# Sliding-window attention and a feed-forward layer on one core: batches 0 and 1 handled by token halves, with a new opening order

## The chip, the core and the metric

The kernel runs on one core of a Trainium2 chip. Its engines are TensorE (PE, with PEld for its weight loads), VectorE (DVE), ScalarE (ACT), GpSimd (POOL) and SyncE (SP, which only issues transfers). The metric is the device time of one execution in microseconds (us). Smaller is better.

## The reference

The input is `q`, `k` and `v` of 8 batches, 8 heads, 576 tokens and 64 numbers per head, all fp32. Each token sees the tokens at a distance of at most 32. The output is that of a feed-forward layer on 4608 tokens (512 to 2048 to 512).

```python
scores = scale * np.matmul(q, k.transpose(0, 1, 3, 2))
mask = np.abs(pos[:, None] - pos[None, :]) <= 32
scores = np.where(mask, scores, -1000000000.0)
attn = softmax(scores)                      # written out in the reference, with + 1e-09
x = np.matmul(attn, v)                      # heads joined: 4608 tokens x 512
h = x @ w_in
out = np.maximum(0.01 * h, h) @ w_out
```

## The kernel before

The whole program is written in the order in which each engine shall work; no scheduler moves anything. Each engine takes its instructions in that order, so a waiting instruction holds up all that stand behind it on its engine.

Heads are taken in 4 pairs (p = 0 to 3), so that a pair fills 128 partitions. Batches 0 and 1 are the "old" ones. Each is split into two halves of 288 tokens, and a step is one half of one pair: steps 0 to 3 are the first half of batch 0, 4 to 7 its second half, 8 to 15 batch 1. For a step, `score(i)` (10 small matmuls for batch 0 at L428, 5 for batch 1 at L435) writes a PSUM tile `ps`, ACT takes the exponential into `e` (L440), POOL multiplies it with a band mask into `prob` (L442), `sums(i)` (L466) adds up the rows on PE and DVE takes the reciprocal (L471, the longest DVE instruction), `product(i)` (L482) multiplies with `v`, and `scaled(i)` (L496, DVE) writes 288 columns of `xT`. There is one `ps`, so that the next score waits for the last exponential. `xT` is cut into 4 chunks of 128 rows, one for each pair. Batches 2 to 7 go another way (blocks of 64 tokens, transposes by DMA), from step 16 on (L380 to L411).

The feed-forward layer takes its tokens in groups. Groups 0 to 3 are the halves of batches 0 and 1 (288 tokens each). For each group there are 16 tiles `f`; a tile is 4 matmuls of 288 columns (`h_mms`, L520) and an ACT instruction (L531) into `gT`. The first 4 tiles of groups 0 and 1 are made chunk by chunk (`h_first`), so that they begin when pair 0 is there. 16 matmuls of 512 columns make one output tile of 128 tokens (`o_pair`, L609, for the first two, `o_tile`, L593, for the others). Between these, a plan with due times (`spend`) sets attention steps; its number `turn` counts the places between the matmuls from `o_pair` on.

In the opening, q and k of a pair come as a tile of 96 partitions with 6 tokens each (`load_qk`, L80, 288 KB per tile), v as two transfers of 144 KB per pair (L104), all issued by SP. They are cast to bf16 (`cast_qk`, L279 and L281), transposed on PE (6 transposes per tile, L327) and evicted by ACT (L335 for q, L341 for k). A first score thus needs both tiles of its pair whole. Queries stand with even and odd tokens apart. For batch 0 the keys are used from where ACT put them, for batch 1 DVE copies them into a block-diagonal tile `kbd` (L359). ACT or DVE cast v into a block-diagonal tile `vbd` (L287, L289). The weights come by 8 transfers that POOL issues: four quarters of w_in (4 tiles `f` each, L675) and four of w_out (L679), each 1 MB in memory, cast to bf16 on the way. `keep_busy` (L622) is matmuls whose result is not used.

`vf` and the tiles of `fload` have one buffer for each pair. Thus batch 1 is loaded when batch 0 has been cast; a POOL memset of one element (L76) holds its first load behind what POOL has done.

The opening's order around the first feed-forward matmuls reads (L744 ff.):

```python
    score(4)
    load_w_out(0)
    h0 = h_first(0)
    h = next(h0)
    keep_busy(h, HALF, 8)
    product(2)
```

Of the kernel before, what the change touches and what calls it, by code (L numbers as in the profile page):

```python
# [9 lines left out]
FP32 = mybir.dt.float32  # L10
# [6 lines left out]
def kernel(  # L17
# [14 lines left out]

    nc = tc.nc
# [12 lines left out]
    EVEN = HALF // 2  # L46
# [22 lines left out]
    def load_qk(b, p, behind=None):  # L69

        for into, src, name in ((qf, q, "qf"), (kf, k, "kf")):
            t = fload.tile([96, 2, RUN * D], FP32, name=f"{name}{p}")
            if behind is not None:
                behind.memset(t[0:1, 0, 0:1], 0.0)  # L76
                behind = None
            heads = src[b, 2 * p:2 * p + 2]
            if b < BY_DMA:
                nc.sync.dma_start(out=t, in_=heads.rearrange("a (p c) d -> p a (c d)", c=RUN))  # L80
            elif into is qf:
# [10 lines left out]

    vbuf = const.tile([128, NPAIR, 10 * D], FP32)
# [7 lines left out]
    def load_v(b, p):  # L101
        t = vf[b, p]
        for a in range(2):
            nc.sync.dma_start(  # L104
                out=t[64 * a:64 * a + 64],
                in_=v[b, 2 * p + a].rearrange("(c p) d -> p c d", p=64),
            )
# [17 lines left out]

    load_qk(0, 0)
    load_qk(0, 1)
    load_v(0, 0)
    load_qk(0, 2)
    load_qk(0, 3)  # L130
    for p in range(1, NPAIR):
        load_v(0, p)


    qb = const.tile([96, NPAIR, RUN, 2, D], BF16)
    kb = const.tile([96, NPAIR, RUN, 2, D], BF16)
# [5 lines left out]
    qT, kbd, vbd, qz, kz, vw, vw_two = [], [], [], [], [], [], []  # L142
    for t, at in zip(sets, (0, NPAIR * S)):
        qT.append(sets[0][:, at:at + NPAIR * S].rearrange("p (n s) -> p n s", n=NPAIR))
# [22 lines left out]
    def clear(t, p):  # L167
# [4 lines left out]

    mask = [const.tile([128, 2, 2, EVEN], BF16, name=f"mask{i}") for i in range(2)]
    nc.vector.memset(mask[0][:, 1, :, 0:16], 0.0)
    nc.vector.memset(mask[1][:, 1, :, 128:EVEN], 0.0)
# [7 lines left out]
        [((0, 0, 48), (2, 48, 64), (4, 112, 32)), ((1, 16, 64), (3, 80, 64))],  # L183
        [((4, 0, 32), (6, 32, 64), (8, 96, 48)), ((5, 0, 64), (7, 64, 64))],
    ]

    win = sets[1][:, N_SET - 384:].rearrange("p (c m i) -> p c m i", c=2, m=3)
    nc.gpsimd.memset(win, 1.0)
    for lo in (0, 64):
# [3 lines left out]
            base=0, channel_multiplier=-1, pattern=[[1, 2], [0, 3], [2, 64]],  # L193
# [3 lines left out]
            base=2 * W, channel_multiplier=1, pattern=[[-1, 2], [0, 3], [-2, 64]],  # L197
        )
    nc.gpsimd.memset(vbd[0][:, 3], 0.0)
    win_f = win.rearrange("p c m i -> p c (m i)")  # L200

    def make_mask(hf):
        lo = (16, 32)[hf]
        nc.gpsimd.tensor_copy(out=mask[hf][:, 0], in_=win_f[:, :, lo:lo + EVEN])
        lo = (16, 0)[hf]
        nc.gpsimd.tensor_copy(out=mask[hf][:, 1, :, lo:lo + 128], in_=win_f[:, :, 0:128])
# [49 lines left out]
    prob = const.tile([128, NPROB, 2, 2, EVEN], BF16)  # L256
# [3 lines left out]
    ps_v = ps[:, P0:P0 + 2 * HALF].rearrange("p (n c i) -> p n c i", n=2, c=2)  # L260
# [14 lines left out]
    def cast_qk(b, p, q_eng=None):  # L275
        for eng, src, dst in ((q_eng or nc.gpsimd, qf, qb), (nc.gpsimd, kf, kb)):
            to, tok = dst[:, p], src[b, p].rearrange("p a (c d) -> p c a d", d=D)
            if eng is nc.scalar:
                eng.activation(out=to, in_=tok, func=AF.Copy)  # L279
            else:  # L280
                eng.tensor_copy(out=to, in_=tok)  # L281

    def cast_v(b, p, on_act=False, heads=range(2), eng=nc.gpsimd):
        for a in heads:
            r = slice(64 * a, 64 * a + 64)
            if on_act:
# [31 lines left out]
    def transposes(b):  # L318

        for p in range(NPAIR):  # L320
            for which, src in (("q", qb), ("k", kb)):
# [17 lines left out]
                else:  # L339
# [5 lines left out]
                    if b == 0:  # L345
                        first_keys.append(kT)
                    else:
                        unplaced.append((b, p, kT))
# [555 lines left out]
```

## Time and profile before

| | |
|---|---|
| time, median of 3 runs (range) | 314.39 us (313.86 to 315.52) |
| time of the profiled execution | 314.13 us |
| span of its profile | 312.3 us |
| PE busy, share of the span | 298.2 us, 95% |
| DVE, ACT, POOL busy | 221.6, 212.6 and 199.1 us |
| PE busy in 0 to 10, 10 to 22, 22 to 40 us | 3.21, 10.03 and 17.64 us |
| first matmul of the feed-forward layer (L520) | 22.07 us |
| transfers of q0 (weights, by POOL) and of q1 (all else) | 4.19 and 44.84 MB written |

Times in a profile count from the start of the span; the time of the run is 1.8 us longer than the span. In the timeline a row is: start, length from the first instruction's start to the last one's end, engine, line, operation, tiles (written from read), shape, count, and in brackets the idle time before it with what ended that. The ends of matmuls are modelled. In the list of transfers the last number is the median time from issue to landing.

### The profile page before, as it was taken

The numbers are of one execution on the slowest core, as the hardware profiler recorded it, in microseconds if no ns is written. First come the engines' busy times: TensorE is split into PE (matmuls) and PEld (weight loads), VectorE is DVE, ScalarE is ACT, GpSimd is POOL, SyncE is SP. The second block draws the span as 40 slices with busy tenths as digits, with TensorE's granted clock in tenths as the row PEclk, the third lists the DMA queues.
The fourth block names the chain that finished last, engine by engine and source line by source line (L and its number), as shares of the span: only waits on it lengthen the run. The fifth ranks groups of instructions, "written<-read, shape, count | busy, mean of one in ns | idle before, by whom it ended". The sixth has DMA issues, their size and how long they took to land.

```text
span 312.3 us, 6748 instructions
## 1 busy us (share of the span) xinstructions
PE 298.2 (95%) x2516; PEld 194.8 (62%) x2545; DVE 221.6 (71%) x290; ACT 212.6 (68%) x434; POOL 199.1 (64%) x250
## 2 busy tenths in 40 slices
PE   1799999999999999999999999999999999999996
PEld 1577775585765858585959585858555555544643
DVE  3688959779768887898789767898679866743000
ACT  7687698583865858585949686858589548842731
POOL 7789936899799999488778357578947622110000
PEclk9999999999999999999999999999999999999999
DMA  8999999998999799989989995797950011001002
GB/s 181 224 217 227 268 249 198 204 216 143 211 216 216 145 266 174 206 174 251 198 145 186 257 230 101 163 209 144 206 129 0 33 67 41 0 36 68 34 28 75
DMA packets 122017, 49.47 MB, mean 158 GB/s; under 512 B 96256, under 2 KB 117504, under 8 KB 121984
## 3 DMA queue, kind: packets, MB, share of 16 engines
q1 hardware_dynamic: 117760, 44.84, 72.7%
q0 software_dynamic: 4224, 4.19, 8.0%
q8 instruction: 20, 0.33, 0.5%
q14 instruction: 13, 0.11, 0.1%
HBM read 36.70 MB, written 9.44 MB: 148 GB/s over the span
## 4 chain that ended last, share of the span: by engine, by line
PE 77%; POOL 10%; DMA 5%; ACT 3%; SPq 2%; issue 2%; DVE 1%; POOLq 0%; ACTq 0%; DVEq 0%
PE mm L520 34%; PE mm L593 31%; PE ps L380 3%; DMA kf<-in_k_dram 2%; PE mm L609 2%; POOL prob L387 2%; PE s L398 2%; POOL kb L281 2%; PE x L398 2%; POOL qb L281 2%; DMA set<-kb 1%; ACT set L287 1%; POOL prob L442 1%; DMA vbuf<-in_v_dram 1%; SPq L80 1%
## 5 line engine op out<-in xcount | busy, mean ns | idle before, releaser
L520 PE MATMUL mm<-xT,w_in_bf 128*128 128x256 bf16 (+3 forms) x956 | 133.2, 294 | 0.4
L593 PE MATMUL mm<-w_out_bf,gT 128*128 128x512 bf16 (+2 forms) x537 | 122.5, 373 | 1.3
L407 DVE RECIPROCAL r<-r 128x256 f32<-128x256 f32 (+1 forms) x56 | 94.9, 1696 | 37.3 <-ACT r L406 36.9
L520 PEld LDWEIGHTS <-w_in_bf 128*128 128x128 bf16 x960 | 91.4, 98 | 30.6 <-issue 0.6
L387 POOL TENSOR_TENSOR prob<-e,band 128x512 bf16<-128x512 bf16 (+1 forms) x56 | 62.6, 1117 | 56.0 <-ACT e L385 54.6
L593 PEld LDWEIGHTS <-gT 128*128 128x128 bf16 x560 | 52.0, 98 | 54.1
L531 ACT ACTIVATE gT<-mm 128x288 bf16<-128x288 f32 (+2 forms) x112 | 49.8, 479 | 12.3 <-PE mm L520 9.6
L385 ACT ACTIVATE e<-ps 128x512 bf16<-128x512 f32 (+1 forms) x56 | 32.4, 579 | 27.7 <-PE ps L380 27.0
L598 ACT ACTIVATE o_sb<-mm 128x512 f32<-128x512 f32 (+2 forms) x35 | 20.5, 585 | 38.5 <-PE mm L593 38.2
L554 ACT ACTIVATE gT<-mm 128x512 bf16<-128x512 f32 x64 | 35.7, 596 | 5.5 <-PE mm L520 4.2
L471 DVE RECIPROCAL r<-s 128x288 f32<-128x288 f32 x16 | 31.2, 1950 | 2.9 <-PE s L466 2.8
L281 POOL CAST kb<-kf 96x768 bf16<-96x768 f32 x32 | 27.2, 851 | 9.2 <-DMA kf<-in_k_dram 8.1
L411 DVE TENSOR_TENSOR xT<-x,r 64x256 bf16<-64x256 f32 (+1 forms) x56 | 24.3, 435 | 3.3
L411 DVE TENSOR_TENSOR xT<-s,r 64x256 bf16<-64x256 f32 (+1 forms) x56 | 24.3, 434 | 3.3
L442 POOL TENSOR_TENSOR prob<-e,mask 128x576 bf16<-128x576 bf16 x16 | 20.3, 1273 | 5.9 <-ACT e L440 4.9
L315 DVE COPY set<-kT 64x576 bf16<-64x576 bf16 x48 | 21.4, 446 | 2.1 <-DMA kT<-qb 1.2
L380 PEld LDWEIGHTS <-set 128*128 128x128 bf16 x216 | 16.7, 98 | 9.6 <-DMA set<-kb 0.4
L380 PE MATMUL ps<-set 128*128 128x128 bf16 x216 | 21.4, 219 | 0.2 <-DMA set<-kb 0.2
L281 POOL CAST qb<-qf 96x768 bf16<-96x768 f32 x24 | 19.6, 819 | 0.8 <-DMA qf<-in_q_dram 0.8
L294 POOL CAST set<-vbuf 128x640 bf16<-128x640 f32 x24 | 17.2, 716 | 3.1 <-DVE r L407 1.7
L398 PEld LDWEIGHTS <-set 128*128 128x128 bf16 x432 | 18.0, 98 | 0.5
L295 POOL CAST set<-vbuf 64x512 bf16<-64x512 f32 x24 | 14.8, 615 | 1.5
(84 smaller groups left out, 237.0 us busy)
## 6 DMA issues: line engine op xcount, KB each, us to landing
qf<-in_q_dram SPq DMA_DIRECT2D x32, 288.0 KB, 5.9
kf<-in_k_dram SPq DMA_DIRECT2D x32, 288.0 KB, 6.6
out_dram<-o_sb SPq DMA_DIRECT2D x35, 256.0 KB, 2.7
vbuf<-in_v_dram SPq DMA_DIRECT2D x15, 256.0 KB, 4.7
vbuf<-in_v_dram SPq DMA_DIRECT2D x16, 144.0 KB, 7.0
w_in_bf<-in_moe_w_in_dram POOLq DMA_DIRECT2D x4, 512.0 KB, 8.2
w_out_bf<-in_moe_w_out_dram POOLq DMA_DIRECT2D x4, 512.0 KB, 15.5
vbuf<-in_v_dram SPq DMA_DIRECT2D x10, 192.0 KB, 4.5
```

The costliest lines, as they stand in the source:

```text
L281: eng.tensor_copy(out=to, in_=tok)
L380: nc.tensor.matmul(sc[:, :, w], kz[b % 2][:, p, 64 * m:64 * m + 128], tok[:, :, :, at:at + 32], start=True, stop=True,)
L385: nc.scalar.activation(out=e[:, 0:n], in_=ps[:, lo:lo + n], func=AF.Exp, scale=scale)
L387: nc.gpsimd.tensor_mul(pr, e[:, 0:n], band.rearrange("p w c i -> p (w c i)")[:, 0:n])
L398: nc.tensor.matmul(x[:, a, w], vw[b % 2][:, p, m, a:a + 2].rearrange("p n d -> p (n d)"), pr[:, a, w], start=True, stop=True,)
L407: nc.vector.reciprocal(r[:, 0:n], r[:, 0:n])
L411: nc.vector.tensor_mul(xT[rows, p, t0:t0 + n].rearrange("p (w i c) -> p w c i", i=32, c=2), x[rows, a].rearrange("p (w c i) -> p w c i", c ...
L471: nc.vector.reciprocal(r, s)
L520: nc.tensor.matmul(h[:, 0:n], w_in_bf[:, c, ts(f, 128)], xT[:, c, t0:t0 + n], start=(c == 0), stop=(c == DMC - 1),)
L531: nc.scalar.activation(out=to, in_=h, func=AF.Prelu, alpha=0.01)
L554: nc.scalar.activation(out=gT[:, f - 1:f + 1, t0:t0 + 256], in_=hh.rearrange("p (f t) -> p f t", f=2), func=AF.Prelu, alpha=0.01,)
L593: nc.tensor.matmul(o[:, lo:hi], gT[:, f, t0:t0 + 128], w_out_bf[:, f, lo:hi], start=(f == 0), stop=(f == FFC - 1),)
```

## The change

For batches 0 and 1, a load is now one half of one pair: 48 rows of q and 64 (first half) or 32 (second half) rows of k in one tile of 112 or 80 partitions (`load_half`), by two transfers. v comes as 5 blocks of 64 tokens and later the other 4. All first halves of a batch are loaded ahead of its second halves. One cast, 6 transposes, one eviction and, for batch 1, two DVE copies serve a half tile. Tokens stand in natural order in `qk`, the masks, `prob` and `gT`. `score` leaves out the masking, which `mask_out` does where it is called, for step 0 on DVE. The opening is a new list: `warm_up` (37 matmuls of 128 columns) in place of `keep_busy`; both masks at the start; two clears (`clear_half(0, 0, .)`) on DVE at the start, which stood on ACT and POOL beside `o_pair`; two tiles (`h_first(0, 2)`) begun early in place of four; the four w_in transfers each behind one POOL masking or cast; the four w_out transfers and the loads of batch 1 among the second half's steps; POOL's making of `band`, two clears and DVE's `clear_half(1, .)` at other places. In batch 1, half tiles are transposed behind tiles 5, 8, 11 and 14 of group 1, and at turns 6, 8, 11 and 13 (before: pairs behind tiles 7 and 11 and at turns 1 and 5). In the last lines of the diff, `transpose_part` is the transposes of a half tile and its two copies into `kbd`, and `cast_part` is the cast of the half tile of pair 2, then 3, on DVE.

```diff
+    QROWS, KROWS = 48, (64, 32)
+    def load_half(b, p, hf, behind=None):
+        t = load_tile(p, ("qf", "kf")[hf])
+        if behind is not None:
+            behind.memset(t[0:1, 0, 0:1], 0.0)
+        k0, kn = 384 * hf, KROWS[hf]
+        for src, row, t0, n in ((q, 0, HALF * hf, QROWS), (k, QROWS, k0, kn)):
+            nc.sync.dma_start(
+                out=t[row:row + n],
+                in_=src[b, 2 * p:2 * p + 2, t0:t0 + RUN * n].rearrange(
+                    "a (p c) d -> p a (c d)", c=RUN),
+            )
+        halves[b, p, hf] = t[0:QROWS + kn]
...
-    load_qk(0, 0)
-    load_qk(0, 1)
-    load_v(0, 0)
-    load_qk(0, 2)
-    load_qk(0, 3)
+    load_half(0, 0, 0)
+    load_half(0, 1, 0)
+    load_v(0, 0, 0, 5)
+    load_half(0, 2, 0)
+    load_half(0, 3, 0)
     for p in range(1, NPAIR):
-        load_v(0, p)
+        load_v(0, p, 0, 5)
+    for p in range(NPAIR):
+        load_half(0, p, 1)
+        load_v(0, p, 5, NB)
...
+    def transposes(b, p, hf, tag="mm"):
+        n = QROWS + KROWS[hf]
+        pool = mmps if tag == "mm" else xps
+        tp = pool.tile([128, RUN, 112], BF16, name="tp", tag=tag)[:, :, 0:n]
+        for c in range(RUN):
+            nc.tensor.transpose(
+                tp[:, c], (qb, kb)[hf][0:n, p, c].rearrange("p a d -> p (a d)"), ident[0:n, 0:n],
+            )
+        at = halves_at(hf)
+        nc.scalar.activation(
+            out=qk[b][:, p, at:at + RUN * n].rearrange("p (i c) -> p i c", c=RUN),
+            in_=tp.rearrange("p c i -> p i c"), func=AF.Copy,
+        )
...
     def h_out(g, f, h):
         t0, n = GROUPS[g]
-        to, h = gT[:, f, t0:t0 + n], h[:, 0:n]
-        if g < 2 * BY_DMA:
-            to = to.rearrange("p (i c) -> p i c", c=2)
-            h = h.rearrange("p (c i) -> p i c", c=2)
-        nc.scalar.activation(out=to, in_=h, func=AF.Prelu, alpha=0.01)
+        nc.scalar.activation(out=gT[:, f, t0:t0 + n], in_=h[:, 0:n], func=AF.Prelu, alpha=0.01)
...
-        if i == OLD - 2:
-            for a in range(2):
-                clear_half(0, 2, a, nc.gpsimd)
+        if OLD <= i < OLD + NPAIR:
+            clear_half(1, (i - OLD) // 2 * 2, i % 2, nc.vector)
...
+    warm_up(24)
+    clear_half(0, 0, 0, nc.vector)
+    clear_half(0, 0, 1, nc.vector)
+    cast_half(0, 0, 0, nc.vector)
+    make_mask(0)
+    make_mask(1)
+    cast_half(0, 1, 0, nc.vector)
+    transposes(0, 0, 0)
+    warm_up(5)
+    score(0, nc.vector)
+    transposes(0, 1, 0)
+    warm_up(8)
+    cast_v(0, 0, nc.vector, hi=5)
+    cast_half(0, 2, 0, nc.gpsimd)
+    load_w_in(0, 512)
+    mask_out(0)
+    score(1)
+    sums(0)
+    transposes(0, 2, 0)
+    product(0)
+    scaled(0)
+    mask_out(1)
...
+    score(3)
+    h0 = h_first(0, 2)
+    h = next(h0)
+    sums(2)
+    transposes(0, 0, 1)
+    mask_out(3)
+    load_w_in(1024, 1536)
+    product(2)
+    scaled(2)
+    next(h0)
+    cast_v(0, 3, nc.scalar, nc.gpsimd, hi=5)
+    cast_half(0, 1, 1, nc.scalar)
+    score(4)
+    sums(3)
+    next(h0)
+    transposes(0, 1, 1)
+    mask_out(4)
+    load_w_in(1536, 2048)
+    cast_half(0, 2, 1, nc.scalar)
+    cast_half(0, 3, 1, nc.gpsimd)
+    product(3)
+    scaled(3)
+    next(h0)
+    score(5)
+    sums(4)
+    next(h0)
+    transposes(0, 2, 1)
+    cast_v(0, 0, nc.scalar, nc.gpsimd, lo=5)
+    mask_out(5)
...
+    f = 2
+    for i, n in zip(range(NPAIR, 2 * NPAIR), (2, 3, 4, 5)):
+        for f in range(f, f + n):
+            h_tile(0, f)
+        f += 1
+        if i < 6:
+            score(i + 2)
+        product(i)
+        scaled(i)
         if i < 7:
             sums(i + 1)
+        if i == 4:
+            transposes(0, 3, 1)
+        if i < 6:
+            mask_out(i + 2)
+        if i < 7:
+            cast_v(0, i - 3, nc.scalar, nc.gpsimd, lo=5)
+            load_w_out(i - 4)
+        if i == 4:
+            halves_of(1, 0, nc.gpsimd)
+    load_w_out(3)
+    for p in range(NPAIR):
+        load_v(1, p, 0, 5)
+    halves_of(1, 1)
+    for p in range(NPAIR):
+        load_v(1, p, 5, NB)
+    for p in range(NPAIR):
+        nc.gpsimd.memset(kbd[1][:, p], 0.0)
+    clear_half(0, 2, 0, nc.vector)
+    clear_half(0, 2, 1, nc.vector)
+    cast_half(1, 0, 0, nc.vector)
+    cast_half(1, 1, 0, nc.vector)
+    for p in (0, 1):
+        nc.gpsimd.memset(vbd[1][:, p], 0.0)
     for p in (2, 3):
         nc.vector.memset(vbd[1][:, p], 0.0)
     for _ in h_first(1):
         pass
+    for _ in band_parts:
+        pass
...
     for f in range(4, FFC):
         h_tile(1, f)
-        if f in (7, 11):
-            second_pair((f - 7) // 4)
+        if f in (5, 8, 11, 14):
+            transpose_part((f - 5) // 3)
+            if f < 11:
+                cast_part((f - 5) // 3 + 2)
         if f == 13:
             score(8)
+            mask_out(8)
```

310 lines of the change are left out of this document (117 added, 193 removed).

## The prediction

> **What bounds the kernel now.** I read the page's slices first, then its list of transfers, the stretches, the waits of PE, the timeline of the first 46 us, and the chain.
>
> ```profile
> PE   1799999999999999999999999999999999999996
> w_in_bf<-in_moe_w_in_dram POOLq DMA_DIRECT2D x4, 512.0 KB, 8.2
> w_out_bf<-in_moe_w_out_dram POOLq DMA_DIRECT2D x4, 512.0 KB, 15.5
> ```
>
> ```profile
> 22.00:62.00 40.00, 39.18 (x360) 26.40 (x362) 32.33 (x42) 30.43 (x63) 29.78 (x33) 1.00 1.18 231
> 62.00:104.50 42.50, 42.10 (x364) 28.89 (x367) 33.47 (x42) 28.52 (x67) 39.10 (x55) 1.00 1.08 194
> ```
>
> The fields are the stretch, its length, then busy time of PE, PEld, DVE, ACT and POOL, clock, DMA share and GB/s. From 22 us on PE is the bound: it stands only 0.82 of 40 us, then 0.4 of 42.5 (there POOL is busy 92%). So the change can gain only ahead of 22 us (PE busy 13.2 of 22), and can lose anywhere.
>
> ```profile
> 4.14 1.53 DVE L281 CAST qb<-qf 96x768 bf16<-96x768 f32 x1 [1.79 <-DMA qf<-in_q_dram]
> 8.30 0.66 PE L428 MATMUL ps<-set,kT 64*64 64x96 bf16 x10
> 9.87 1.27 POOL L442 TENSOR_TENSOR prob<-e,mask 128x576 bf16<-128x576 bf16 x1 [0.57 <-POOL kb L281]
> 11.09 0.93 POOL L675 DMA_DIRECT2D w_in_bf<-in_moe_w_in_dram  x1
> 18.83 0.43 PE L428 MATMUL ps<-set,kT 64*64 64x96 bf16 x10
> 22.07 1.14 PE L520 MATMUL mm<-xT,w_in_bf 128*128 128x288 bf16 x8
> 23.54 1.55 POOL L679 DMA_DIRECT2D w_out_bf<-in_moe_w_out_dram  x2
> 35.52 2.53 DVE L281 CAST qb<-qf 96x768 bf16<-96x768 f32 x2
> 38.11 1.15 DVE L788 MEMSET set<- 128x576 uint32 x2
> 41.12 0.56 DVE L281 CAST qb<-qf 96x768 bf16<-96x768 f32 x1
> 44.09 1.03 PE L609 MATMUL mm<-w_out_bf,gT 128*128 128x512 bf16 x3
> ```
>
> In these timeline rows the opening is a chain: cast, transposes, eviction, score, masking, sums, and each link waits for the one before. The same DVE cast takes 1.53 us beside a POOL memset and 0.56 us without one. Ten score matmuls take 0.66 us early, 0.43 at 18.83.
>
> ```profile
> PE tp L327 <- DVE qb L281: 6.4, 2, 5.7
> PE s L466 <- POOL prob L442: 1.4, 2, 1.2
> PE ps L380 <- DMA set<-kb: 0.2, 1, 0.2
> ```
>
> The waits of PE (sum, number, longest) say the same: 6.4 of its idle time is for the first casts. Places to gain are the opening's chain and, at most 0.6 us, the wait for a transposing DMA at 104.5.
>
> **A. The chain of batch 0's first half.** A half tile is 112 rows of 3 KB, 336 KB where a q tile had 288. Four tiles land between 4.14 and 8.48 (the DVE and POOL casts that wait for them), 1.45 us each, so the first casts can start at about 4.4 instead of 4.14. But POOL's memset L199 (4.21, 1.06) remains, and the cast should again end near 5.7: no gain. The two clears now on DVE (0.54 each at 7.83 and 8.53) fit into its 1.79 us of waiting. Then 6 transposes instead of 12 and one eviction (0.65 us for 576 columns, about 0.73 for 672): score(0) at 7.3 instead of 8.30. Its masking goes to DVE, for which there is no row: POOL needs 1.27; DVE's scaled copy of half as many columns 0.46; I take 0.7, nearer to DVE's row. sums(0) then stands at 9.6 (before 11.20). Two more rounds of exponential, masking and the PSUM tile `ps` at 2.4 to 2.5 us each (before 3.3 and 4.0, with two casts per pair between them) give sums(2) at 14.6 instead of 18.50, and product(2) at 15.8.
>
> **B. The first matmul of the layer.** It needs the first quarter of w_in. POOL issues that behind its cast of pair 2's half tile, which lands at about 8.5 (1.2 MB from the start, at the 0.2 MB per us of the tiles above), and casts for 0.82: issue 9.3 instead of 11.09. With the page's median of 8.2 us it lands at 17.5. The other end: landings of quarters three and four lie 2.5 us apart in the trace, so a quarter alone could be there at 13; and if loads crowd it, 19. So PE stands about 1.7 us, and the first matmul comes at 17.5 instead of 22.07: 4.5 us earlier.
>
> The Trainium skill ("DMA: Bandwidth & Descriptors", section "Queues, rings and completion order") says that each DMA engine goes round its queue rows packet by packet. By that rule POOL's quarter shares the engines with SP's loads as long as these last, as the 8.2 us show; the sum stays as it is, and without the rule it would be that of rival 2.
>
> **C. Group 0.** Those 4.5 us are not kept, because the second half's steps are now the chain. mask(4) runs on POOL from about 19.0 to 20.3; behind it stand on POOL the fourth w_in issue (0.8), a cast of a k tile (0.82) and half a v cast (0.4), then mask(5) (1.27): 23.7. sums(5) follows at 23.8. From there PE has work: 12 tiles of 4 matmuls at 0.49 (16 matmuls from 38.90 to 40.86), 0.24 for each of six sums and products, 0.33 for a score, 0.22 for transposes, 7.9 in all, and some 0.3 of waits: group 1's first matmul at 32.0, before 34.04. Gain 2.0.
>
> **D. Group 1 up to the output pair.** Before: 16 tiles 7.84, six tiles of transposes 1.56, a score 0.24, one wait for ACT 0.42, in all 10.06; the rows say 10.0 (34.09 to 44.09). Now: 7.84, four half tiles at 0.29 (0.26 for 96 rows), 0.24, 0.33: 9.6, so 41.6. But the transposes now come from tile 5 on, and their casts stand on DVE behind scaled(7) (to 33.5), the clears L254 that were on POOL (1.3 beside its memsets), two casts (2.53 at 35.52, beside POOL's memsets), two memsets (1.15), copies. The first half tile is cast at 36.1 and wanted at 35.3; the third at about 39.8 to 40.5, wanted at 39.5 after that wait. I take 1.0 of waiting (0.5 to 1.7): 42.6 instead of 44.09, gain 1.5. Four smaller half tiles (0.22 each) follow later where one pair (0.51) did: gain 1.1 carried on.
>
> **E. w_out.** The four issues stand on POOL behind mask(6), mask(7) and v casts: about 26, 28.8, 30 and 30.8, where they were 23.54, 24.34, 26.35 and 28.45. Before, a quarter was there 10.2 us after the first issue and the others 4.65 us apart (landings in the trace, 33.75 to 46.90). Now 34.5 to 36.2 for the first, so the third between 43.8 and 45.5; `o_pair` wants it at 44.6, the fourth at 49.7. Wait 0 to 1.6, I take 0.5.
>
> **F. The output tiles up to 62 us.** ACT gets 16 v casts of 0.4 instead of 8 of 0.69 and four more evictions of about 0.55, less a clear of 1.2: hidden, ACT is busy 30 of 40. DVE's key copies (384 columns, 0.33 each by 0.45 for 576) move to turns 6 to 13, between its reciprocals: 0.3 of waits, an estimate.
>
> **G. After 62 us.** POOL loses two clears (1.06 each) and three parts of `band` (about 2.0) there, where it runs at 92%: I give 0.3 of the 0.6 us at 104.5. DVE gets four clears, 2.8 us, over four steps at 79% busy: hidden; if not, up to 0.7.
>
> **The rest** costs nothing on the path: `warm_up`'s matmuls stand ahead of the first cast and in waits of A; natural order changes only how ACT and POOL walk their tiles, which the PE-bound stretches hide (L531 takes 0.48 us, a tile on PE 0.49; were it slower in the new order, ACT would set the pace, but the order gets plainer); the doubled number of SP's load issues has slots of 0.4 us free.
>
> **Sum.** -1.1 (A to D) +0.5 (E) +0.3 (F) -0.3 (G) = -0.6 on the profiled execution of 314.13: 313.5. The median of the runs is 0.26 above the profiled one: 313.8. A measurement of this kernel can tell about 0.5%, 1.57 us, from no change; so this is "the same" (312.8 to 316.0).
>
> **Rivals.** 1. *The late w_out becomes the wait (slower).* If batch 1's loads, issued at nearly the same moment, take more of the DMA than before (the first w_in quarter took 8.2 us under load against 2.5 apart when nothing else ran), the third quarter lands near 48 instead of 45, and `o_pair` stands 3.4 us instead of 0.5: 316.7. For it: DMA share 1.18 in 22 to 62. Against: both requests start later together. It decides from a landing of the third quarter at 47.3.
>
> 2. *The opening's gain is kept (faster).* If the first quarter comes by 15.8, as the 2.5 us apart would allow, PE does not stand; the POOL chain of C starts 1.2 us earlier, group 1 at 31.0; DVE's queue then waits 0.5 rather than 1.0, and w_out comes in time: 313.8 - 1.0 - 0.5 - 0.5 = 311.8. Against: while batch 0 is loaded the trace shows 8 us, not 2.5.
>
> 3. *A slow PE after the stand.* If PE stands longer than 1.7 us, what follows may go at the early price (0.66 for 0.43) for a few us; PE isn't alone the bound there, so about +0.7: 314.5. It would want first matmuls of the layer at twice 0.12 us each.
>
> The Trainium skill ("TensorE: Matmul & The Clock Gate", section "What's actually happening") has a clock at half rate until about 3.4 us of sustained work, and again after such an idle window. The rows 0.66 and 0.43 agree in kind; by it `warm_up` would make score(0) and score(1) some 0.2 us shorter each, and the sum 313.6 at best.
>
> 4. *No gain in the opening*: if the score of step 1 or 2 waits for ACT (two evictions, an exponential and casts in one queue), sums(2) is near 18 again and group 1 starts at 33.5: with D to G 315.3.
>
> **How the numbers follow.** Forecast 0.42, rival 1 0.18, rival 2 0.25, rival 3 0.06, rival 4 0.09. Around 313.8 the open costs (D 0.5 to 1.7, E 0 to 1.6, F and G some 0.7 either way) make about 1.3 each way, which is the likeliest case's own range, 312.5 to 315.1; 0.06 of its 0.42 fall below 312.8. Faster: 0.25 + 0.06 = 0.31. Slower: rival 1, half of rival 4 (its 315.3 with the same open costs) and 0.01 of rival 3: 0.24. Same: the rest, 0.45. The range reaches over rival 2 with 1.0 of the open costs below it, and over rival 1 with 0.5 above it: 310.8 to 317.2.
>
> **What would show it.** Right: first score near 7.3, sums(0) at 9.6, first layer matmul at 17 to 18.5 with a wait on w_in ahead of it, group 1's first matmul near 32.0, o_pair's near 42.6 with waits for DVE's casts before it, group 2's first within 1 us of before's 61.8. Wrong: a first layer matmul before 16.5 or after 20, a third w_out quarter after 47, a PE wait over 2 us anywhere between 22 and 62, or a PE wait after 62 that before does not have; and a reciprocal chain on DVE that sets the pace from 62 on, for which I put nothing.

## The result and the profile after

The changed kernel takes 325.96 us (median of 4 runs, 323.91 to 326.59), the kernel before 314.22 us (4 runs, 313.86 to 315.52): ratio 1.0355 [1.0298, 1.0411]. It is slower by 11.7 us where 313.8 us were forecast. The profiled execution took 325.49 us and has a span of 323.8 us (before: 314.13 and 312.3).

The page of after, its slices and its weight transfers:

```profile
PE   5659987997899999999999999999999999999996
PEclk9758999999999999999999999999999999999999
w_in_bf<-in_moe_w_in_dram POOLq DMA_DIRECT2D x4, 512.0 KB, 6.7
w_out_bf<-in_moe_w_out_dram POOLq DMA_DIRECT2D x4, 512.0 KB, 10.9
```

Before, the row of PE was full from the third slice (of 8.1 us) on; now it has holes up to the eleventh, and PE's clock is reduced in slices two to four. Both weight loads land faster than before (8.2 and 15.5 us then), so they are not what is missing. The stretches of after (length, busy PE, PEld, DVE, ACT, POOL, clock, DMA share, GB/s) give their size:

```profile
0.00:10.00 10.00, 5.54 (x71) 4.50 (x71) 5.06 (x16) 7.50 (x9) 6.96 (x17) 1.00 0.64 169
10.00:22.00 12.00, 6.12 (x69) 4.16 (x69) 6.89 (x6) 6.20 (x11) 6.55 (x9) 0.60 1.08 196
22.00:62.00 40.00, 35.52 (x328) 24.24 (x326) 29.96 (x43) 27.88 (x65) 29.07 (x35) 0.95 0.96 186
62.00:104.50 42.50, 39.04 (x333) 25.72 (x330) 31.25 (x41) 27.68 (x65) 30.67 (x39) 1.00 1.05 199
```

PE now stands 4.5 us of the 40 from 22 on (before 0.8), and 3.5 of the next 42.5 (before 0.4). From 22 us on no other engine is fuller than before, so none of them became the bound: they wait too. In the first 10 us the DMA engines are emptier than before, where this stretch reads

```profile
0.00:10.00 10.00, 3.21 (x34) 2.35 (x35) 4.76 (x14) 7.45 (x9) 6.96 (x17) 1.00 0.91 194
```

so there the loads are short of transfers given out, not of DMA engines (share 0.64 against 0.91). The waits of PE (sum, number, longest) say what it stood for:

```profile
PE tp L345 <- ACT kb L292: 4.3, 1, 4.3
PE tp L345 <- POOL kb L294: 2.0, 1, 2.0
PE tp L345 <- DVE qb L294: 1.9, 2, 1.2
```

Apart from the 2.2 us that PE waits ahead of its very first matmul, these are the longest of the opening and of batch 1, and all three are transposes (`tp`) that wait for the cast of a half tile: two of a second half (`kb`), one of batch 1's first half (`qb`). The timeline of after shows what those casts wait for themselves:

```profile
6.96 0.43 PE L434 MATMUL ps<-set 64*64 64x96 bf16 x10 [0.54 <-ACT set L349]
7.27 3.96 SPq L116 DMA_DIRECT2D vbuf<-in_v_dram  x6
11.92 0.64 SPq L98 DMA_DIRECT2D kf<-in_k_dram  x1
19.10 0.84 ACT L292 ACTIVATE kb<-kf 80x768 bf16<-80x768 f32 x1 [4.45 <-DMA kf<-in_k_dram]
19.99 0.58 PE L345 MATMUL tp<-ident,kb 80*128 80x80 bf16 x6 [4.31 <-ACT kb L292]
20.82 0.69 PE L530 MATMUL mm<-xT,w_in_bf 128*128 128x288 bf16 x2
37.12 9.95 SPq L116 DMA_DIRECT2D vbuf<-in_v_dram  x8
47.12 1.27 SPq L98 DMA_DIRECT2D kf<-in_q_dram  x1
54.28 0.82 POOL L294 CAST kb<-kf 80x768 bf16<-80x768 f32 x1 [2.77 <-DMA kf<-in_k_dram]
55.16 0.39 PE L345 MATMUL tp<-ident,kb 80*128 80x80 bf16 x6 [2.05 <-POOL kb L294]
59.94 0.54 SPq L77 DMA_DIRECT2D qf<-in_q_dram  x1
```

An SP row gives when transfers are given out, and the number in brackets how long an engine stood and for what. The second half of pair 0 is given out by SP at 11.27 (q) and 11.92 (k) as transfers 17 and 18, lands at 17.13 and 19.01, is cast by ACT at 19.10 and transposed at 19.99, and only then can the first matmul of the layer follow at 20.82, although its quarter of w_in (issued at 10.04) had landed at 16.16. In batch 1 the same happens behind eight v transfers: SP gives out the first second half at 47.12. And the loads of batch 2, which stand behind all of this in SP's queue, begin at 59.94; in the trace of before they begin here:

```profile
49.10 0.58 SPq L82 DMA_DIRECT2D qf<-in_q_dram  x1
```

So batch 2's loads start 10.84 us later. More than half of this arises ahead of batch 1, whose first load is given out at 25.19 before and at 31.64 after:

```profile
25.19 0.32 SPq L80 DMA_DIRECT2D qf<-in_q_dram  x1
31.64 0.32 SPq L98 DMA_DIRECT2D qf<-in_q_dram  x1
```

SP has nothing to give out from 24.49 to 31.64, because the POOL memset that releases batch 1 comes at 31.53 (before: 25.07). So 6.45 us are the later release, and 4.39 are the giving out of batch 1, which takes 28.30 us for 32 transfers where it took 23.91 for 16.

How far after lags behind before at fixed points of the program, from the two timelines:

| point | before, us | after, us | lag | forecast |
|---|---|---|---|---|
| first layer matmul | 22.07 | 20.82 | -1.2 | -4.5 |
| group 1's first | 34.1 | 37.2 | +3.1 | -2.0 |
| first of `o_pair` | 44.1 | 48.1 | +4.0 | -1.5 |
| group 2's first | 62.1 | 68.7 | +6.6 | -0.3 |
| an output tile at the end of the stretch from 62 us | 100.6 | 111.7 | +11.1 | |
| end of the span | 312.3 | 323.8 | +11.5 | -0.6 |

From 112 us on the lag hardly changes: nearly all of the loss lies in the opening and its echo.

### The profile page after: what moved, and what is told of

It is laid out like the page before. It is cut to its first block, busy times and chain, and to the rows that moved or that the text cites. A ratio compares the mean times of both kernels' runs of the same rounds, so it can differ in the third digit from the quotient of the medians.

```text
span 323.8 us, 6901 instructions
## 1 busy us (share of the span) xinstructions
PE 301.9 (93%) x2561; PEld 195.6 (60%) x2561; DVE 225.7 (70%) x303; ACT 213.1 (66%) x444; POOL 197.3 (61%) x251
## 4 chain that ended last, share of the span: by engine, by line
PE 67%; DMA 13%; POOL 8%; SPq 5%; ACT 3%; issue 2%; DVE 1%; POOLq 0%; ACTq 0%; DVEq 0%
PE mm L601 30%; PE mm L530 29%; DMA vbuf<-in_v_dram 6%; DMA kf<-in_k_dram 6%; PE ps L386 3%; POOL prob L393 2%; PE s L404 2%; SPq L128 2%; PE x L404 2%; DMA kT<-qb 2%; SPq L98 2%; SPq L116 2%; POOL prob L452 1%; POOL kb L294 1%; POOL qb L294 1%
## 5 line engine op out<-in xcount | busy, mean ns | idle before, releaser
L530 PE MATMUL mm<-xT,w_in_bf 128*128 128x256 bf16 (+3 forms) x960 | 135.3, 295 | 0.1
L601 PE MATMUL mm<-w_out_bf,gT 128*128 128x512 bf16 (+2 forms) x560 | 124.6, 373 | 0.0
L606 ACT ACTIVATE o_sb<-mm 128x512 f32<-128x512 f32 (+2 forms) x35 | 20.5, 585 | 36.2 <-PE mm L601 35.9
L294 POOL CAST kb<-kf 96x768 bf16<-96x768 f32 (+1 forms) x29 | 24.0, 830 | 6.5 <-DMA kf<-in_k_dram 5.3
L452 POOL TENSOR_TENSOR prob<-e,mask 128x576 bf16<-128x576 bf16 x15 | 19.2, 1277 | 12.1 <-ACT e L446 11.7
L294 POOL CAST qb<-qf 96x768 bf16<-96x768 f32 (+1 forms) x25 | 20.6, 822 | 4.2 <-DMA qf<-in_k_dram 2.0
L349 ACT ACTIVATE set<-tp 128x672 bf16<-128x672 bf16 (+1 forms) x16 | 10.4, 650 | 9.4 <-PE tp L345 9.2
## 6 DMA issues: line engine op xcount, KB each, us to landing
w_out_bf<-in_moe_w_out_dram POOLq DMA_DIRECT2D x4, 512.0 KB, 10.9
```

Of the source, the lines that this page charges most:

```text
L294: eng.tensor_copy(out=to, in_=src)
L530: nc.tensor.matmul(h[:, 0:n], w_in_bf[:, c, ts(f, 128)], xT[:, c, t0:t0 + n], start=(c == 0), stop=(c == DMC - 1),)
L601: nc.tensor.matmul(o[:, lo:hi], gT[:, f, t0:t0 + 128], w_out_bf[:, f, lo:hi], start=(f == 0), stop=(f == FFC - 1),)
```

## The experiments

Theory 1: the doubled number of SP's transfers is the cost; SP gives them out one after another, so that everything behind them in the queue is late. Theory 2: their order is the cost (second halves behind v, batch 2 behind both). Theory 3: the casts that ACT now does in order hold up its exponentials. Lags are those of the table, against the kernel before.

**split_before**: the kernel before, with every load of batches 0 and 1 in two pieces.

```diff
-                nc.sync.dma_start(out=t, in_=heads...)
+                for lo in (0, 48):
+                    nc.sync.dma_start(out=t[lo:lo + 48], in_=rows[lo:lo + 48])
...
+            for lo, hi in ((0, 5), (5, NB)):
+                nc.sync.dma_start(out=t[64 * a:64 * a + 64, lo:hi], in_=rows[:, lo:hi])
```

> The kernel before, with every load of batches 0 and 1 cut into two transfers (q and k tiles into two times 48 rows, v into 5 and 4 blocks), nothing else moved. Theory 1 (count: SP gives out transfers one after the other, 0.45 to 0.6 us each, and the ninth waits until the first has landed, so half-sized transfers keep fewer bytes under way): batch 0 lands some 3 us or more later, batch 1 and so batch 2 too, 317 to 322 us. Theory 2 (place: the second halves stand behind v and behind a POOL memset at 31.5) and theory 3 (ACT stands on a cast) have no part in this kernel: 313.5 to 315.5 us.

Measured: 324.24 us (324.07 to 324.36), ratio 1.0329 [1.0304, 1.0354]. Same bytes, same order, same compute, and 10 us are lost. SP is done with batch 0 at 20.98 instead of 15.34 and begins batch 1 at 28.68 instead of 25.19. The first layer matmul lags by 3.9, group 1 by 10.8, and that stays. In its waits of PE:

```profile
PE x L483 <- ACT set L288: 7.4, 3, 3.6
```

That is `product` waiting for the casts of v, which are the last of batch 0's loads. PE's mean clock is 0.72 from 22 to 40 us, so a slower PE may be part of the 10 us; that was not separated. For the kernel before theory 1 holds, more strongly than expected.

**whole_v**: after, with v loaded whole (24 transfers per batch instead of 32).

```diff
-    load_v(0, 0, 0, 5)
+    load_v(0, 0)
...
-        load_v(0, p, 5, NB)
```

> The kernel after, with v of batches 0 and 1 loaded whole again (8 transfers per batch in place of 16), at the place of the first parts. Theory 1 (count): SP is done with batch 0 some 4 us earlier, batch 1's second halves are issued near 42 instead of 47.1 and batch 2's first load near 53 instead of 59.9; 318 to 322 us. Theory 2 (place): 0.4 MB more of v, about 2 us, now stands ahead of batch 0's second halves, so the first matmul of the layer comes near 22 instead of 20.8 and the time is 325 to 328 us.

Measured: 325.88 us (325.14 to 326.98), ratio 1.0386 [1.0355, 1.0416]. Fewer transfers and no gain: with v whole, more bytes stand ahead of the second halves, and batch 1's second halves are given out only at 53.95. In its waits of PE:

```profile
PE tp L344 <- ACT kb L291: 6.3, 1, 6.3
PE tp L344 <- POOL kb L293: 5.9, 1, 5.9
```

So in after the number alone is not it either: what stands behind what counts (theory 2).

**act_late**: after, with ACT's casts of second halves behind the exponential that follows.

```diff
-    cast_half(0, 0, 1, nc.scalar)
     score(3)
+    cast_half(0, 0, 1, nc.scalar)
```

> The kernel after, with the three ACT casts of batch 0's second halves each put behind the next exponential (steps 3, 4, 5) in place of ahead of it. Theory 3 (ACT stands 4.4 us on the cast of pair 0's second half, and the exponential of step 3 behind it): exponential of step 3 at 14.8, first layer matmul at 16.5 to 17.5, group 1's first matmul near 34 instead of 37.2, 321 to 323 us. Theories 1 and 2 (the loads set the pace): the same first two marks, but step 4's score stays near 21.4 and group 1's first matmul within 0.7 of 37.2; 325 to 326.5 us.

Measured: 327.15 us (325.81 to 328.06), ratio 1.042 [1.0386, 1.0455]; first layer matmul at 20.5, group 1's lag 5.4. ACT's order is not the cause: the exponential of step 3 now starts at 15.51 instead of 19.84, and the cast still stands for the same load, until 18.73 (19.10 in after). Theory 3 falls.

**b1_early**: after, with batch 1's loads released some 7 us earlier and its second halves ahead of v.

```diff
     load_w_in(1536, 2048)
+    halves_of(1, 0, nc.gpsimd)
...
-        if i == 4:
-            halves_of(1, 0, nc.gpsimd)
...
+    halves_of(1, 1)
     for p in range(NPAIR):
         load_v(1, p, 0, 5)
-    halves_of(1, 1)
```

> The kernel after, with batch 1's first halves released behind the fourth w_in issue (near 25 instead of 31.5) and its second halves ahead of the first parts of v. Theory 2 (place): first cast of batch 1 not waited for, the 2 us wait for a second half's cast beside the output tiles is gone, batch 2's first load near 54; 317 to 320 us. Theory 1 (count): SP still needs as many issues, batch 2's first load stays within 3 us of 59.9, and what the second halves gain the v parts lose: 322 to 326 us.

Measured: 321.1 us (319.86 to 322.5), ratio 1.0232 [1.0189, 1.0275]. The wait of 2.05 at 55.16 is gone, batch 2 begins to load at 55.61, and the lags are +2.7, +3.6, +4.0 and +5.9 at the end. The time lies between the two ranges expected. The earlier release and the new order of batch 1's loads are together worth 4.9 us of the 11.7 (4.4, if each kernel is compared with the kernel before of its own session); which of the two does it was not separated.

**joined** and **joined_early**: whole_v with q or k of two pairs in one transfer, then the same with second halves among v and batch 1 early. Both have no more transfers than before (or hardly more: 18 and 16).

```diff
-                out=t[row:row + n],
-                in_=src[b, 2 * p:2 * p + 2, ...]
+                out=whole[row:row + n, p:e].rearrange("r p a e -> r (p a) e"),
+                in_=src[b, 2 * p:2 * e, ...]
```

> As whole_v (v of batches 0 and 1 loaded whole, second halves behind it), but with the q and k rows of two pairs in one transfer each: pairs 2 and 3 in the first half of batch 0, and both times two pairs in its second half and in batch 1. 18 transfers for batch 0 and 16 for batch 1, where whole_v has 24, the kernel after 32 and the kernel before 16. Theory 1 (the number of transfers): SP has given out batch 0 by about 14 instead of 19.7, its last part lands some 3 us earlier, batch 1's second halves still wait behind v; 320 to 323 us. Theory 2 (place alone): 325 to 327 us, as whole_v.

> As joined, with the second halves of batch 0's pairs 0 and 1 ahead of v of pairs 2 and 3, and batch 1's halves released behind the fourth w_in issue, its second halves ahead of v. Theories 1 and 2 together (number and place of the transfers are the whole loss): group 1's first matmul at 33 to 34.5, no wait for a cast over 1 us beside the output tiles, 311.5 to 315 us. If something else in the change costs as well (more work for ACT and DVE ahead of tile 16, the later w_out): 316 to 319 us.

Measured: 330.22 us (329.2 to 330.7), ratio 1.0514 [1.0484, 1.0544], and 322.12 us (321.83 to 322.38), ratio 1.0262 [1.0234, 1.0291]. The first was expected at 320 to 323 and is the worst of all. A joined transfer lands only when both pairs are there, and batch 1's second halves still stood behind v: `o_pair` lags by 8.0, group 2 by 16.0. With the order mended 8 us come back, though the time is above both ranges expected: the first w_in quarter is issued at 11.75 (POOL's cast of pair 2 ahead of it waits for the joined tile until 10.98), lands at 20.95, and holds PE 2.7 us. Fewer, larger transfers are no remedy where the first user needs a part.

**tiny_before**: before, with a transfer of 8 rows of 32 bytes behind each load of batch 0.

```diff
+                if b == 0:
+                    tiny()
```

> The kernel before, with one more transfer of 8 rows of 32 bytes behind each of batch 0's 16 loads; nobody uses the data. It adds 16 transfers and no bytes to speak of. Theory 1a (each transfer costs SP about 0.45 us to give out, whatever its size): the last load of batch 0 is given out some 5 us later than 15.3, first layer matmul at 24 to 27, 316.5 to 320 us. Theory 1b (what counts is the bytes under way in the eight places; tiny transfers free theirs at once): less than 1.5 us, 313.5 to 315.5 us.

Measured: 325.48, 324.19, 323.36 and 317.6 us, median 323.77. Sixteen transfers of 256 bytes make every execution slower, the shortest by 3.6 us and the others by 9.3 to 11.5; their price can't be read more closely than that. The queue of SP in the profiled one:

```profile
1.28 0.38 SPq L101 DMA_DIRECT2D tiny_buf<-in_q_dram  x1
1.70 0.33 SPq L80 DMA_DIRECT2D kf<-in_k_dram  x1
21.42 0.54 SPq L101 DMA_DIRECT2D tiny_buf<-in_q_dram  x1
29.24 0.33 SPq L80 DMA_DIRECT2D qf<-in_q_dram  x1
```

A transfer of next to no bytes takes SP 0.34 to 0.54 us, one of 288 KB 0.31 to 0.40. It also takes up a place: SP gives out its 13th transfer at 7.20, when the 5th, eight before it, has landed at 7.19, the 15th at 8.29 (the 7th landed at 8.27) and the 17th at 9.22 (9.20). With every second place taken by 256 bytes, only four loads are under way. The last v of batch 0 lands at 32.37 (before 21.45), batch 1 starts at 29.24 (25.19), and group 1 lags by 11.9. So a transfer has a cost that is not that of its bytes; how much of it is SP's time and how much the place is not separated. Why one of the four runs lost only 3.6 us is open; the profile is of the longest, where PE's clock is 0.62 from 22 to 40 us. A reduced clock that does not always come would fit; that was not shown.

**after_little_v** and **before_little_v**: only pair 0's v is loaded and serves all pairs, in after and in before.

```diff
     def load_v(b, p, lo=0, hi=NB):
+        if p > 0:
+            return
```

> The kernel after, with only pair 0's v of batches 0 and 1 loaded; the casts of pairs 1 to 3 read pair 0's v. That leaves out 12 of 32 transfers and 0.9 of 3.5 MB in each of the two batches; casts, matmuls and order stay. Theory: the loads are what costs. Then batch 0's last half tile lands 6 us or more earlier than 26.1, batch 2's first load is given out near 50 instead of 59.9, and the time is 312 to 316 us. If the new order of steps on PE, POOL and ACT costs by itself, it stays at 318 us or more.

> The kernel before with the same left out (pair 0's v only, 6 of 16 transfers and 0.9 MB fewer in each of batches 0 and 1). The loads are near the pace here too (DMA share 1.25 in 10 to 22): first layer matmul 1 to 3 us earlier than 22.07, 311 to 313.5 us. If nothing but matmuls and chains bounds it: 313.5 to 315 us.

Measured: 326.13 us (323.42 to 326.46), ratio 1.0347 [1.0284, 1.041], and 314.61 us (313.99 to 316.12), ratio 1.001 [0.999, 1.0031]. Before gains nothing from fewer loads: it was not bound by them, against the 311 to 313.5 expected. In after the opening becomes what was forecast: first layer matmul at 16.9 (forecast 17.5), group 1 at 32.6 (forecast 32.0). Its total says nothing, since 8.6 us are lost behind group 2's first matmul (65.3), mostly by the edit's own doing: the cast of pair 3 reads the place that batch 2's v is loaded into, and waits 8.3 us for that load.

**after_half_v**: the same with v of pairs 0 and 2, which avoids that.

```diff
+        if p % 2:
+            return
```

> The kernel after, with v of batches 0 and 1 loaded for pairs 0 and 2 only (the casts of pairs 1 and 3 read those); 8 of 32 transfers and 0.6 MB fewer in each batch. after_little_v had its group 1 at 32.5, but its last part stood 9 us on batch 2's v, because its cast of pair 3 read a place that batch 2 had taken; here it doesn't. Theory: batch 0's late second halves cost the 3 us at group 1, and batch 2's late loads the last 5 us. Then first layer matmul near 17, group 1 at 32.5 to 34, group 2 near 65, and less than 2 us lost after 62; 316 to 319 us. If the loss after 62 comes from the moved clears on DVE and POOL: it stays near 5 us there, 320 to 323 us.

Measured: 318.45 us (318.34 to 318.7), ratio 1.012 [1.0078, 1.0162]. With 24 transfers instead of 32 per batch, and fewer bytes, 7.5 of the 11.7 us are back (8.1 against the kernel before of its own session): first layer matmul at 17.0, group 1 at 33.5 (lag -0.55), batch 2's first load at 51.50, and only 0.2 us is lost behind group 2's first matmul. What is left arises between group 1's first matmul and `o_pair` (lag 3.8). Its rows there:

```profile
32.93 4.05 POOL L792 MEMSET set<- 128x1152 bf16 x4
35.53 5.33 DVE L296 CAST qb<-qf 112x768 bf16<-112x768 f32 x2
39.92 0.47 PE L347 MATMUL tp<-ident,qb 112*128 112x112 bf16 x6 [2.99 <-DVE qb L296]
```

Two casts on DVE take 5.33 us beside POOL's clears, and PE waits 3.0 for them. Right after this stand the granted clock is 0.5 from 40.30 to 43.72, and 12 matmuls take 3.01 us that take 1.70 afterwards. These 3.0 and 1.3 make up nearly all of the 4.4 us by which this part is longer than before. In this run that is the price of step D, sized at 0.5 to 1.7.

**both_early** and **score5**: b1_early with batch 0's second halves among its v; then `score(5)` also ahead of `product(3)`.

```diff
+    load_v(0, 1, 0, 5)
+    load_half(0, 0, 1)
+    load_v(0, 2, 0, 5)
+    load_half(0, 1, 1)
...
+    score(5)
     product(3)
     next(h0)
-    score(5)
```

> As b1_early, with the second halves of batch 0 among the first parts of v (pair 0's behind v of pair 1, pair 1's behind v of pair 2, the others behind v of pair 3); the number of transfers stays. Place theory: the 2.8 us that ACT stood on pair 0's second half are gone, first layer matmul at 17 to 18, group 1's first matmul 1.5 to 2.5 us ahead of 36.8, 318 to 320 us. Number theory (SP gives out one per 0.63 us): v of pairs 2 and 3 now comes as much later, group 1's first matmul stays within 1 us, 320 to 322 us.

> As both_early, with step 5's score on PE ahead of step 3's product instead of behind it. In the kernel after a step of the second half takes 3.0 to 3.3 us, because score, sums, reciprocal, product and the next score stand in one row on PE. If that row is what sets group 0's pace: group 1's first matmul 1 to 2 us earlier than in both_early, the time 1 to 2 us shorter. If the loads set it: within 0.5 us of both_early.

Measured: 320.7 us (319.14 to 321.59), ratio 1.0191 [1.0146, 1.0235], and 320.9 us (320.22 to 322.48), ratio 1.021 [1.0167, 1.0252]; neither differs from b1_early by more than the runs do. The first layer matmul comes at 17.6 and 17.4, as forecast, but in both_early v is now late (PE waits 3.4 in two waits for POOL's casts of it), and group 1 lags by 4.8. Whatever is put ahead in the full queue pushes something else back. In score5's profile group 1 comes 2.7 us earlier than in both_early's, but its span is only 0.8 us shorter: the lead is lost behind group 2's first matmul, and batch 2's first load is given out at nearly the same time (57.08 and 57.56).

**memsets**, **fewer** and **fewer_plus**: b1_early with POOL's clears of `kbd` among the w_out issues; b1_early with v whole and second halves among it (24 transfers); and fewer with both the clears moved and `score(5)` early.

```diff
             load_w_out(i - 4)
+            nc.gpsimd.memset(kbd[1][:, i - 4], 0.0)
...
-    load_v(0, 0, 0, 5)
+    load_v(0, 0)
```

> As b1_early, with POOL's four clears of kbd one by one behind the w_out issues of the last four steps, where they stood in one row behind all of them (36.2 to 40.6, beside DVE's two casts of batch 1, 2.3 us for two that take 0.56 each alone). Theory (contention of DVE's casts with POOL's clears): the two casts take 1.2 to 1.6 us, the wait of 1.2 us for the third cast goes, from group 1's first matmul to the output pair 9.8 to 10.2 us instead of 10.8; time 319 to 320.5 us. If the two that stay (vbd, 1.2 each) are enough to hold DVE: same as b1_early, 321 us.

> As b1_early, with v whole (8 transfers per batch instead of 16, 24 in all instead of 32) and batch 0's second halves between the v transfers. Theory 1 with 2: by SP's 0.63 us per transfer, batch 0 is given out by 15.6 instead of 23.6; pair 0's second half lands by 16, first layer matmul near 17.5, group 1's first matmul at 32.5 to 35 instead of 36.8; 316 to 319.5 us. If 0.2 MB per us of DMA is the limit and not the number: within 1 us of 321.

> fewer, memsets and score5 together: 24 transfers per batch in the order of need, POOL's clears of kbd away from DVE's casts, step 5's score ahead of step 3's product. If loads, clears and the row of steps are all that the change lost: group 1 at 32 to 34, output pair at 42 to 44, group 2 within 1 us of before's 61.8, 312.5 to 315.5 us. If batch 1's v, now last in the queue, or batch 2's loads still come late: 316 to 318 us.

Measured: 321.56 us, ratio 1.0217 [1.0182, 1.0253]; 322.1 us, 1.0236 [1.0179, 1.0293]; 321.07 us, 1.0204 [1.0163, 1.0244]. None gains on b1_early. In memsets PE's waits for DVE's casts rise from 1.9 to 2.8 us, and from group 1 to `o_pair` it takes 13.6 where b1_early takes 10.9: the two casts take 4.51 us beside the clears that remain. In fewer the time is what was expected if the bytes per us and not the number of transfers are the limit (within 1 us of 321). In fewer_plus, which is above both ranges expected, whole v lands later, and PE waits 3.2 us at 19.5 for this cast:

```profile
18.96 0.44 POOL L296 CAST set<-vbuf 64x320 bf16<-64x320 f32 x1 [3.55 <-DMA vbuf<-in_v_dram]
```

Number, order and clears as changed here do not make up the loss together; what the best arrangement of this change would take stays open.

**half_v_act_casts**: after_half_v, with the first two casts of batch 1 on ACT.

```diff
-    cast_half(1, 0, 0, nc.vector)
-    cast_half(1, 1, 0, nc.vector)
+    cast_half(1, 0, 0, nc.scalar)
+    cast_half(1, 1, 0, nc.scalar)
```

> As after_half_v (v of pairs 0 and 2 only), with batch 1's first two half tiles cast by ACT in place of DVE. Theory (DVE is held by POOL's row of clears, 5.3 us for two casts): ACT casts them in 0.84 each, the wait of 3.0 us for the first transposes of batch 1 falls under 1 us, output pair near 44.5 to 45 instead of 47.8, 314.5 to 316 us. If batch 1's loads were the late thing: the wait stays, 318 us.

Measured: 318.21 us (316.39 to 320.28), ratio 1.0131 [1.0085, 1.0177]: no gain. PE's wait for DVE's casts falls from 3.7 to 0.7, but ACT now stands for the loads (0.99 and 1.01 us ahead of the two casts, at 37.15 and 39.00), PE waits 2.3 for ACT's tiles, and the DVE copies of the keys are held until 43.4 behind POOL's making of `band`. From group 1 to `o_pair` it takes 13.4 us, where after_half_v takes 14.4 and before 10.0, and again the granted clock is 0.5 for a while (40.52 to 43.94). So the slow casts and the late landing of batch 1's first halves both limit there; their split is not settled.

**before_clear_later**: before, with one POOL clear (L199) behind the second w_in issue, where it no longer lies beside the first DVE cast.

```diff
-    nc.gpsimd.memset(vbd[0][:, 3], 0.0)
     win_f = ...
...
     load_w_in(512, 1024)
+    nc.gpsimd.memset(vbd[0][:, 3], 0.0)
```

> The kernel before, with POOL's clear at L199 (4.21 to 5.27 us, beside which DVE's first cast takes 1.53 us instead of 0.56) moved behind the second w_in issue. Theory (contention): first transposes at 4.8 instead of 5.73, first score near 7.4 instead of 8.30; the first layer matmul hangs on other links too, so 0 to 1 us: 312.8 to 314.3 us. If the first cast is not held by that clear: no change in these marks and 314 to 315 us.

Measured: 313.73 us (313.07 to 315.15), ratio 0.9983 [0.9958, 1.0007]: the same time. Its first cast and first score:

```profile
4.05 0.56 DVE L280 CAST qb<-qf 96x768 bf16<-96x768 f32 x1 [1.70 <-DMA qf<-in_q_dram]
8.31 0.66 PE L427 MATMUL ps<-set,kT 64*64 64x96 bf16 x10
```

The cast takes 0.56 instead of 1.53 us with the clear away, which shows the clear as its cause; but the score also needs POOL's cast of the keys, and stays at 8.3. No kernel here beats the one before.

## Why the prediction was wrong, step by step

**What bounds before** was read rightly: PE from 22 us on, little to gain, much to lose. before_little_v confirms that its loads are no bound.

**A** held in size up to sums(2): score(0) at 6.96 (forecast 7.3), sums(0) at 9.19 (9.6), its masking on DVE 0.46 us (I took 0.7), sums(2) at 15.02 (14.6). Then it failed: product(2) came at 20.4, not 15.8. I followed only first half tiles. `transposes(0, 0, 1)` stands on PE ahead of product(2), and its cast on ACT ahead of exponential 3; both wait for a second half that SP gives out 17th and 18th. PE stood 4.31 us there.

**B** named the wrong wait. w_in's quarter landed at 16.16, earlier than the 17.5 I put, and nobody was ready for it. With lighter loads the first layer matmul stands at 16.9 to 17.0, and with the same loads in another order at 17.6 (both_early), so the size was right and the missing term was SP's queue. The failing sentence is in **The rest**: "the doubled number of SP's load issues has slots of 0.4 us free". There are no free slots: in after the first 16 transfers are given out from 0.83 to 11.23 without a gap, 0.65 us each. split_before prices such a doubling at 10 us in the kernel before. It is not a price for each transfer: in after, 24 in place of 32 with the same bytes gained nothing (whole_v, fewer), so the order and the bytes ahead count as well.

**C** put 6.3 us from the first layer matmul to sums(5) and 8.2 from there to group 1. Measured are 8.1 and 8.3: the second part is as I described it. The first is 1.8 longer: POOL's cast of pair 3's second half, which I had ahead of mask(5) at 0.82, stands for its load until 26.22, so that mask(5) starts at 27.58; and score and sums rows take 0.66 instead of 0.43 up to 25 us.

**D** was right in size in after: 10.9 us from group 1 to `o_pair`, where the sums of C and D make 10.6, with a wait of 1.2 for DVE's casts. But its cost depends on where the casts fall: in after POOL and DVE interleave, and two casts take 2.28; in after_half_v, beside POOL's clears, they take 5.33 and PE waits 3.0. The term (0.5 to 1.7) rested on one row of before, 2.53, with other work beside it.

**E** put the issues at 26 to 30.8, and they came 4.7 to 5.1 us later; the quarters of before also lie 4.38 us apart on the mean (33.75 to 46.90), not 4.65. The third one landed at 46.9, later than I put, but `o_pair` was later still (48.1), and no wait arose: in that E was lucky.

**F and G** looked only at engines. The loads that the change moves were not followed past group 0. Batch 1's second halves stand behind eight v transfers (wait 2.05 at 55.16), and batch 2's behind all: 59.94 instead of 49.10, of which the later release of batch 1 alone makes 6.45. The loss behind group 2's first matmul goes with how far ahead of it batch 2's first load is given out: 4.9 us are lost in after (8.7 ahead), 4.7 in act_late (8.7), 3.5 in score5 (8.3), 1.9 in b1_early (10.4), 1.8 in both_early (10.3), and at most 0.7 in the other runs, where it is 12.4 or more; before has 13.0. Only after_little_v, with its own wait for v, does not fit. No edit moved batch 2's loads alone, so this is not shown to be the cause. G's 0.3 of gain is not to be seen beside it.

By the table, the error of 12.2 us is made up of 3.3 at the first layer matmul (A, The rest), 1.8 up to group 1 (C), 0.4 up to `o_pair` (D, E), 1.4 up to group 2 (F) and 5.3 after it (G). These are lags read off the timelines, and late loads stand behind most of them: SP's queue is full, and POOL releases batch 1 later. Only the 4.9 us of batch 1's release and order and the 7.5 of the v loads are shown by an edit of after, and the two overlap, since with less v batch 2's loads start earlier too (51.50).

**The rivals.** Rival 1 had the sign, but its place was wrong: no wait for w_out. Rival 2 did not come about; its condition (PE not waiting for w_in) was met, its gain not. Rival 3's slow PE came, but not in its order: score(0) to score(2) took the short 0.43, then the granted clock was 0.5 from 12.36 to 26.01, and the sums at 12.33 already took 0.64. PE's stand of 4.31, from 15.68 to 19.99, lies inside this time and did not begin it. Rival 4's loss of the opening's gain came, but by loads: the scores of steps 1 and 2 were not late, as sums(2) at 15.02 shows, and act_late moved ACT's casts without gain. None of the four was the queue that issues the loads.

The Trainium skill ("DMA: Bandwidth & Descriptors", section "Rules for kernel authors") says to coalesce small transfers, under 64 KB being mostly overhead, and not to split one by partition halves, since both halves go over the same engines. The runs agree in sign and go further: pieces of 64 to 144 KB cost 10 us here (split_before). Joining beyond what the first user needs cost more than it gave (joined, 1.0514).

## What to carry to other kernels

Count the transfers of each issuing queue, not only their bytes, and follow a moved load through every later load of its queue, the next batch's too: here 16 more transfers per batch cost 10 us in the kernel before although bytes and compute were the same. Look also at when each batch's loads are released: 6.45 us of batch 2's delay came from there. When a step is split so that its first half comes sooner, look for the first instruction of the second half in each engine's order, for that one set the time here. Where a cast is costed from a row, look what stood beside it in that row.

## What the runs showed of the hardware

- A transfer of 256 bytes takes SP as long to give out (0.34 to 0.54 us) as one of 288 KB (0.31 to 0.40, both in tiny_before). In the traces SP also stops when eight are out: in after it gives out no transfer from 17.81 to 19.03, and goes on when the k half of pair 0 lands at 19.01, the one eight before. Whether the chip or the way this program is built sets the eight is not shown.
- In after SP's transfers land late while a weight quarter of POOL's is under way: while the first quarter was (10.04 to 16.16), a transfer given out at 10.61 landed at 16.46, and none of SP's landed between 12.27 and 16.46.
- A cast on DVE takes 0.56 us alone, 1.53 beside one POOL clear, and two take 5.33 beside a row of POOL clears without gaps, while these clears keep their 1.0 us each (after_half_v). DVE's own clears (0.54 us) are not lengthened there. The Trainium skill ("SBUF — State Buffer", section "Who interferes with whom") says that a DVE instruction in a 2-port mode, which a cast can enter, and a GpSimd instruction exclude each other: whichever is issued first has the shared ports for the whole instruction, and the other is blocked. The rows agree that they exclude each other: the first cast of before ends 0.40 us after the clear at 4.21 does, and in after_half_v the two casts end only behind several clears. They do not show who comes first: by the trace that cast of before starts at 4.14, ahead of the clear, and still ends after it.
- A wait of PE can cost more than its length: in after_half_v a stand of 2.99 us that ends at 39.92 is followed by a granted clock of 0.5 from 40.30 to 43.72. A long stand is not needed for that: in after the clock falls to 0.5 at 12.36, when PE's waits had been short (busy 3.94 of the 6.70 us from 5.60 to 12.30), and ten score matmuls take 0.66 us until 25 us instead of 0.43.
